# First tile in one DMA with its mean split over ScalarE and VectorE, and the third weight chunk loaded ahead of the third tile: a start-up change in a linear-attention and bilinear-GLU kernel

## The chip, the cores and the metric

The kernel runs on one core of one Trainium2 chip. The metric is the device time in microseconds (us) of one execution, as the median of several runs; the span in a profile, from the first to the last instruction, is 1.8 to 2.1 us shorter.

## The reference

Four layers follow one another on 2048 rows of 1024 bf16 values: linear attention (32 heads of 32), a bilinear GLU (inner width 3584), and both again, each on a layer-normalised input and added to its input. Only the first lines matter for the change: the layer norm of the first rows and the k part of the first product.

```python
def _layernorm(x, axis=-1, eps=1e-5):
    m = jnp.mean(x, axis=axis, keepdims=True)
    v = jnp.var(x, axis=axis, keepdims=True)
    return (x - m) / jnp.sqrt(v + eps)
...
    qkv = (x @ wqkv) ...            # x: [2048, 1024], wqkv: [1024, 3072]
    phi = lambda t: jnp.where(t > 0, t + 1, jnp.exp(t)) + 1e-6
    pq, pk = phi(q), phi(k)
...
    x = x + _A_ref(_layernorm(x, axis=-1), A_wqkv, A_wo)
    x = x + _B_ref(_layernorm(x, axis=-1), B_w_gate, B_w_up, B_w_down)
    # and the same two once more
```

## The kernel before

The rows are handled in 16 tiles of 128. `X[:, t, :]` is tile t, `wkv[:, k, :]` is chunk k (128 rows of the weight, 1024 columns). Every piece of the start is 256 KB: one tile of x or one chunk of the weight. All of them are issued by SyncE in this order; the first tile comes in two halves:

```python
    for c in range(2):
        load(X[:, 0, c * NB:(c + 1) * NB], x_view[:, 0, c * NB:(c + 1) * NB])
    load_x(1)
    for k in range(2):
        load_k(k, k + 1)
    load_x(2)
    for k in range(2, 4):
        load_k(k, k + 1)
    load_x(3)
    for k in range(4, 8):
        load_k(k, k + 1)
```

For the first four tiles the division by the standard deviation is put off to the exponential after the product, so TensorE needs only x minus its mean, turned round (the first three tiles are transposed on TensorE and copied out of PSUM, its output memory, by VectorE and ScalarE; the fourth by a DMA). `idle(9)` gives TensorE nine matmuls on zeros while nothing has landed. `k_part(t, a, b)` adds chunks a to b of tile t, two matmuls of 128x512 per chunk:

```python
            idle(9)
            ln_stats(0)                          # two bn_stats, bn_aggr on VectorE; rstd on GpSimd
            centre(0, stat[0][0][:, 0:1])        # x - mean on VectorE
            nc.scalar.activation(out=junk[:], in_=X[:, 1, :], func=ACT.Copy, scale=1.0 / D, accum_out=mean1[:])
            turn_pe(0, 2)
            take(nc.vector.tensor_copy, 0, 0, 0, 2)
            take(nc.scalar.copy, 0, 1, 2, 8)
            centre(1, mean1[:])
            k_part(0, 0, 1)
            turn_pe(1, 4)
            take(nc.vector.tensor_copy, 1, 0, 0, 4)
            take(nc.scalar.copy, 1, 1, 4, 8)
            ln_stats(2)
            centre(2, stat[2][0][:, 0:1])
            k_part(1, 0, 1)
            for k in range(1, 3):
                for t in range(2):
                    k_part(t, k, k + 1)
            turn_pe(2, 8)
            for t in range(2):
                k_part(t, 3, 4)
            take(nc.scalar.copy, 2, 0, 0, 8)
            ...                                   # tile 3, loads of the query weights and of tiles 4 to 15
            ln_stats(1)
            ...                                   # the other k parts, then three more layers
```

## Time and profile before

| | before |
|---|---|
| time, median of 3 runs | 1625.13 us (1624.67 to 1625.25) |
| span of the profiled run | 1623.0 us |
| TensorE busy | 1618.8 us |

These are lines of the page of the kernel before: its head, the line of busy time of TensorE and its neighbours, and the shares by engine of the chain that ended last.

```profile
span 1623.0 us, 18701 instructions
PE 1618.8 (100%) x8129; PEld 736.3 (45%) x8129; DVE 609.7 (38%) x895; ACT 287.4 (18%) x387; POOL 54.5 (3%) x136
PE 100%; DVE 0%; issue 0%
```

TensorE is the limit, and nothing else is. From about 10 us on its matmuls start 0.216 us apart (read up to 120 us). So all that a change of the start can win lies in the first 10 us. Here is the timeline of TensorE there, kernel before. The columns are start and duration in us, engine, line of the kernel, operation, output and inputs, shapes and how many instructions were merged; in brackets stands how long the engine sat idle before and what ended that. (The last line is cut off by the window.)

```profile
1.17 4.02 PE L172 MATMUL ps<-xT 128*128 128x512 bf16 x9 [1.17 <-DVE xT L167]
5.05 1.03 PE L408 MATMUL pt<-ident,R 128*128 128x128 bf16 x8
5.87 0.83 PE L202 MATMUL ps<-W,xT 128*128 128x512 bf16 x2
6.58 0.62 PE L408 MATMUL pt<-ident,R 128*128 128x128 bf16 x8
7.50 2.33 PE L202 MATMUL ps<-W,xT 128*128 128x512 bf16 x10 [0.30 <-DVE xT L411]
9.67 0.61 PE L408 MATMUL pt<-ident,R 128*128 128x128 bf16 x8
10.11 4.26 PE L202 MATMUL ps<-W,xT 128*128 128x512 bf16 x19
```

The three lines at L408 are the transposes of the first, second and third tile. Each transpose lasts longer than the distance to the next, since they are pipelined, so read starts: the last of the second tile's transposes starts at 6.98, a further one could start 0.056 us after it, and the next matmul starts at 7.50. That is a hole of 0.46 us, of which the profile counts 0.30 as idle. It waits for VectorE's copy of the second tile. Two smaller holes, about 0.06 us each, stand before the first and the second tile's transposes. Together they are 0.6 us.

VectorE's timeline of the same stretch, kernel before:

```profile
2.94 1.29 DVE L181 BATCH_NORM_STATS2 st<-X 128x6 f32<-128x512 bf16 x2 [1.82 <-DMA X<-in_A_x_dram]
4.26 0.21 DVE L183 BATCH_NORM_AGGREGATE mv<-st 128x2 f32<-128x12 f32 x1
4.51 0.48 DVE L395 TENSOR_SCALAR R<-X,mv 128x1024 bf16<-128x1024 bf16 x1
...
7.02 0.42 DVE L411 COPY xT<-pt 128x512 bf16<-128x512 bf16 x1 [0.49 <-PE pt L408]
7.37 1.29 DVE L181 BATCH_NORM_STATS2 st<-X 128x6 f32<-128x512 bf16 x2
8.69 0.21 DVE L183 BATCH_NORM_AGGREGATE mv<-st 128x2 f32<-128x12 f32 x1
8.93 0.49 DVE L395 TENSOR_SCALAR R<-X,mv 128x1024 bf16<-128x1024 bf16 x1
```

The first three lines are the first tile (its second half landed at 3.47), the last three the third tile, which landed at 7.34: statistics, aggregation, centring, ready at 9.42. TensorE arrived at the third tile's transposes at 9.67, so it did not have to wait for them, by a slack of only 0.2 us.

When a load has landed is read from its semaphore in the trace (the last of its 16 increments). Kernel before, in order of issue: first tile 2.92 and 3.47, second tile 4.83, chunk 0 5.70, chunk 1 6.66, third tile 7.34, chunk 2 8.48, chunk 3 9.14, fourth tile 9.82.

### The profile page before, as it was taken

The page shows a single profiled execution, that of the slowest core. Times are in us where ns is not written, and L with a number is a line of the kernel's source. Part 1 is how long each engine was busy: PE and PEld are TensorE (multiplying, and loading weights), DVE is VectorE, ACT ScalarE, POOL GpSimd, SP SyncE. Part 2 cuts the span into 40 slices and gives each one's busy share as a digit, 9 for nine tenths or more (in the row PEclk, how much of TensorE's full clock was granted, in tenths as well). Part 3 has the DMA queues.
Part 4 walks back from the last instruction along what each step waited for, and adds up shares of the span by engine and source line. Part 5 has one row for each costly group of instructions (what it writes and reads, how often), then busy time and mean ns, then how long its engine had stood idle before and what let it go on. Part 6 is the DMA issues. An engine that isn't in the chain of part 4 may idle for free.

```text
span 1623.0 us, 18701 instructions
## 1 busy us (share of the span) xinstructions
PE 1618.8 (100%) x8129; PEld 736.3 (45%) x8129; DVE 609.7 (38%) x895; ACT 287.4 (18%) x387; POOL 54.5 (3%) x136
## 2 busy tenths in 40 slices
PE   9999999999999999999999999999999999999999
PEld 4444444444444444444444444444444444444444
DVE  6889853212311321243245798432123113211111
ACT  5533201101110110011045222011011101101110
POOL 2100000000000000010000000000000000000000
PEclk9999999999999999999999999999999999999999
DMA  7324855511550452142420258555235306511400
GB/s 237 56 71 99 241 161 175 162 52 56 169 165 0 143 161 86 52 156 64 92 53 1 78 99 256 150 165 162 71 100 172 131 20 175 162 65 65 156 0 26
DMA packets 236065, 182.87 MB, mean 113 GB/s; under 512 B 101584, under 2 KB 216784, under 8 KB 235984
## 3 DMA queue, kind: packets, MB, share of 16 engines
q1 hardware_dynamic: 235984, 181.69, 38.8%
q8 instruction: 63, 1.03, 0.3%
q14 instruction: 18, 0.15, 0.0%
HBM read 153.09 MB, written 4.19 MB: 97 GB/s over the span
## 4 chain that ended last, share of the span: by engine, by line
PE 100%; DVE 0%; issue 0%
PE ps L202 50%; PE ps L526 48%; PE ps L553 1%; PE kv L310 0%; PE ps L172 0%; PE pm L334 0%; PE pt L408 0%; DVE xT L411 0%; DVE X L534 0%; DVE xT L167 0%; PE ps L334 0%
## 5 line engine op out<-in xcount | busy, mean ns | idle before, releaser
L526 PE MATMUL ps<-xT,R 128*128 128x512 bf16 x2432 | 528.5, 379 | 0.0
L526 PEld LDWEIGHTS <-R 128*128 128x128 bf16 x2432 | 238.0, 98 | 286.9
L530 DVE TENSOR_TENSOR R<-gs,ps 128x512 bf16<-128x512 f32 x224 | 153.9, 687 | 533.5 <-ACT gs L529 533.5
L202 PEld LDWEIGHTS <-R 128*128 128x128 bf16 x2248 | 219.9, 98 | 265.3
L529 ACT COPY gs<-ps 128x512 f32<-128x512 f32 x224 | 131.0, 585 | 1040.4 <-PE ps L526 1040.4
L526 PE MATMUL ps<-xT,W 128*128 128x512 bf16 x1152 | 251.6, 379 | 0.0
L202 PEld LDWEIGHTS <-xT 128*128 128x128 bf16 x1536 | 149.2, 98 | 180.0 <-issue 1.8
L202 PE MATMUL ps<-W,xT 128*128 128x512 bf16 x1024 | 225.3, 379 | 0.3 <-DVE xT L411 0.3
L526 PEld LDWEIGHTS <-W 128*128 128x128 bf16 x1152 | 112.7, 98 | 135.9
L202 PE MATMUL ps<-W,R 128*128 128x512 bf16 x744 | 170.7, 379 | 0.0
L534 DVE TENSOR_TENSOR X<-X,ps 128x1024 bf16<-128x1024 bf16 (+3 forms) x34 | 39.4, 1159 | 335.7 <-PE ps L202 326.1
L202 PE MATMUL ps<-R,R 128*128 128x512 bf16 x512 | 112.5, 379 | 0.0
L202 PE MATMUL ps<-PQ,R 128*128 128x512 bf16 x496 | 112.1, 379 | 0.0
L202 PE MATMUL ps<-R,xT 128*128 128x512 bf16 x512 | 110.8, 379 | 0.0
L181 DVE BATCH_NORM_STATS2 st<-X 128x6 f32<-128x512 bf16 x128 | 81.9, 682 | 2.4 <-DMA X<-in_A_x_dram 2.2
L207 ACT ACTIVATE e<-ps 128x1024 bf16<-128x1024 f32 x56 | 57.3, 1024 | 140.2 <-PE ps L202 140.2
L185 POOL TENSOR_SCALAR ve<-mv 128x1 f32<-128x1 f32 x64 | 16.7, 260 | 1328.7 <-DVE mv L183 1328.7
L202 PE MATMUL ps<-GL,R 128*128 128x512 bf16 x248 | 58.6, 379 | 0.0
L202 PE MATMUL ps<-xT,R 128*128 128x512 bf16 x248 | 58.6, 379 | 0.0
L379 DVE TENSOR_TENSOR X<-X,ps 128x1024 bf16<-128x1024 bf16 x32 | 38.5, 1212 | 25.9 <-PE ps L202 25.9
L192 DVE TENSOR_SCALAR R<-X,mv,rstd 128x1024 bf16<-128x1024 bf16 x64 | 33.9, 542 | 23.9 <-POOL rstd L187 23.9
L278 DVE TENSOR_TENSOR tmp<-PQ,GL 128x1024 f32<-128x1024 bf16 x32 | 39.0, 1220 | 6.4 <-ACT GL L271 6.3
(68 smaller groups left out, 436.1 us busy)
## 6 DMA issues: line engine op xcount, KB each, us to landing
R<-in_B_w_gate_dram SPq DMA_DIRECT2D x38, 1024.0 KB, 5.4
R<-in_B_w_up_dram SPq DMA_DIRECT2D x38, 1024.0 KB, 7.2
W<-in_B_w_gate_dram SPq DMA_DIRECT2D x18, 1024.0 KB, 5.3
W<-in_B_w_up_dram SPq DMA_DIRECT2D x18, 1024.0 KB, 7.3
W<-in_A_wqkv_dram SPq DMA_DIRECT2D x10, 1024.0 KB, 6.0
W<-in_B_w_down_dram SPq DMA_DIRECT2D x6, 1024.0 KB, 11.3
PQ<-in_B_w_down_dram SPq DMA_DIRECT2D x4, 1024.0 KB, 7.9
X<-in_A_x_dram SPq DMA_DIRECT2D x15, 256.0 KB, 5.4
```

The lines of the kernel that those rows point to most:

```text
L181: nc.vector.bn_stats(out=st[:, c, :], in_=X[:, t, c * NB:(c + 1) * NB])
L185: nc.gpsimd.tensor_scalar(out=ve[:], in0=mv[:, 1:2], scalar1=1e-5, scalar2=None, op0=ALU.add)
L192: nc.vector.tensor_scalar(out=dst, in0=X[:, t, :], scalar1=mv[:, 0:1], scalar2=rstd[:], op0=ALU.subtract, op1=ALU.mult)
L202: nc.tensor.matmul(out=ps[:, n, :], lhsT=lhsT, rhs=rhs[:, n * NB:(n + 1) * NB], start=start, stop=stop)
L207: nc.scalar.activation(out=e[:], in_=flat(ps), func=ACT.Exp, **sc)
L278: nc.vector.tensor_tensor(out=tmp[:], in0=q, in1=zacc, op=ALU.mult)
L379: nc.vector.tensor_tensor(out=X[:, t, :], in0=X[:, t, :], in1=flat(ps), op=ALU.add)
L526: nc.tensor.matmul(out=ps[:, n, :], lhsT=w[:, k, j * P:(j + 1) * P], rhs=xT[g % 2][:, k, :], start=(k == 0), stop=(k == KD - 1))
L529: nc.scalar.copy(out=gs[:], in_=ps[:, 0, :])
L530: nc.vector.tensor_tensor(out=hT[:, f, :], in0=gs[:], in1=ps[:, 1, :], op=ALU.mult)
L534: nc.vector.tensor_tensor(out=X[:, t, a:b], in0=X[:, t, a:b], in1=ps, op=ALU.add)
L553: nc.tensor.matmul(out=ps[:, 0, 0:b - a], lhsT=hT[:, f, tl * P:(tl + 1) * P], rhs=wd[f][:, a:b], start=(f == 0), stop=(f == KF - 1))
```

## The change

The intent is to let TensorE start its real work earlier. The first tile comes in one DMA instead of two, which also takes one issue out of the queue; its mean is summed in halves by ScalarE and VectorE side by side, and its full statistics are computed later, when only the exponential wants them. Chunks 1 and 2 of the weight are to be there earlier, and two matmuls of the first tile (chunk 1) are moved into the hole at 7.50.

```diff
--- before.py
+++ after.py
@@ -135,14 +135,12 @@
     def load_dn(j):
         load(dn[j], wd_v[:, 4 * j:4 * j + 4, :])
 
-    for c in range(2):
-        load(X[:, 0, c * NB:(c + 1) * NB], x_view[:, 0, c * NB:(c + 1) * NB])
+    load_x(0)
     load_x(1)
-    for k in range(2):
+    for k in range(3):
         load_k(k, k + 1)
     load_x(2)
-    for k in range(2, 4):
-        load_k(k, k + 1)
+    load_k(3, 4)
     load_x(3)
     for k in range(4, 8):
         load_k(k, k + 1)
@@ -413,9 +411,15 @@
             mean1 = small.tile([P, 1], F32, tag="mean1", bufs=1, name="mean1")
             junk = small.tile([P, D], BF16, tag="eb", bufs=3, name="junk")
 
+            half = small.tile([P, 3], F32, tag="half", bufs=1, name="half")
+
             idle(9)
-            ln_stats(0)
-            centre(0, stat[0][0][:, 0:1])
+            nc.scalar.activation(out=junk[:, 0:NB], in_=X[:, 0, 0:NB], func=ACT.Copy, scale=1.0 / D,
+                                 accum_out=half[:, 0:1])
+            nc.vector.tensor_reduce(out=half[:, 1:2], in_=X[:, 0, NB:D], axis=AX.X, op=ALU.add)
+            nc.vector.tensor_scalar(out=half[:, 2:3], in0=half[:, 1:2], scalar1=1.0 / D, scalar2=half[:, 0:1],
+                                    op0=ALU.mult, op1=ALU.add)
+            centre(0, half[:, 2:3])
             nc.scalar.activation(out=junk[:], in_=X[:, 1, :], func=ACT.Copy, scale=1.0 / D, accum_out=mean1[:])
             turn_pe(0, 2)
             take(nc.vector.tensor_copy, 0, 0, 0, 2)
@@ -427,10 +431,10 @@
             take(nc.scalar.copy, 1, 1, 4, 8)
             ln_stats(2)
             centre(2, stat[2][0][:, 0:1])
-            k_part(1, 0, 1)
-            for k in range(1, 3):
-                for t in range(2):
-                    k_part(t, k, k + 1)
+            k_part(0, 1, 2)
+            k_part(1, 0, 2)
+            for t in range(2):
+                k_part(t, 2, 3)
             turn_pe(2, 8)
             for t in range(2):
                 k_part(t, 3, 4)
@@ -441,6 +445,7 @@
             load_q()
             for t in range(4, NT):
                 load_x(t)
+            ln_stats(0)
             ln_stats(1)
             for t in range(2):
                 k_part(t, 4, 6)
```

## The prediction

> **What bounds the kernel.** TensorE. The page gives PE 1618.8 of 1623.0 us busy, and the chain of waits that ends last is 100% PE. From 10.1 us on, the timeline shows matmuls 0.216 us apart (over the first 60 us read) without a gap. The change touches only the first 12 us, so it can win only what PE idles there. By the starts in the timeline: about 0.06 us before the first tile's transposes (5.05 us), 0.06 us before the second tile's (6.58), and about 0.47 us before the matmul at 7.50, which waits for VectorE's copy of the second tile. In all 0.6 us, 0.04% of the span.
>
> **First tile.** Before: its second half is there at about 3.5 us, two statistics of 0.68 us, aggregation 0.21, centring 0.49, done at 4.99. After: I estimate the one DMA lands at 3.1; ScalarE's half takes about 0.65 plus 0.19 us for reading the accumulator (a whole row took 1.06 plus 0.19), VectorE's sum about 0.65 (a 512-wide statistic takes 0.68; the Trainium skill, "VectorE: DVE Perf Modes", lists `tensor_reduce` at the 1x rate only, which no run here shows yet), the combining operation 0.1, centring ends near 4.6. That is 0.4 us earlier, but worth only 0.06: the nine idle matmuls, 0.427 us each, hold PE until 4.99. The Trainium skill ("TensorE: Matmul & The Clock Gate", Part 1) says an idle PE starts at half clock; the trace agrees (0.427 us before about 6.3 us, 0.216 after).
>
> **Reordered matmuls.** The two matmuls of tile 0, chunk 1, move ahead of the wait at 7.50 and fill it (0.43 of 0.47 us). Chunk 1 landed at 6.66 and should now land near 6. With the second tile's transposes 0.1 us earlier, PE would reach the third tile's transposes near 9.1 instead of 9.67.
>
> **What gives it back.** The third tile is now sixth of the 256 KB pieces, not fifth. It landed at 7.34; VectorE needs 2.08 us from there (statistics, aggregation, centring), then PE transposes. The sixth piece landed at 8.48 before; one issue fewer (0.45 us each) and full-size packets bring it forward, and I estimate 7.65, between 7.3 and 8.1. Then its transposes start at about 9.75, against 9.67: PE idles 0.6 us there instead of at 7.5. Break-even is a landing at 7.56.
>
> **Moved.** The first tile's statistics now run after the third centring: rstd about 1 us later than its own need, so the first exponential starts near 14.4, not 13.83. PE does not wait for it. The second half of the query weights landed 22.96, wanted at 23.07: a gain above about 0.1 us needs the fourth tile's centring earlier too.
>
> **Sum.** -0.06 -0.06 -0.43 +0.6, so about 0: **1625.0 us, range 1624.2 to 1625.9**. Chances: faster by over 2% 0.00, within 2% 1.00, slower 0.00. The runs of before already differ by 0.6 us.
>
> **Right or wrong in the profile.** Right: the first transposes start at 4.95 to 5.05; no PE gap near 7.5; a new PE gap of 0.3 to 0.9 us before the third tile's transposes, ended by VectorE's centring, itself waiting for the DMA of the third tile. Wrong: no such gap (third tile landed by 7.2; then about 0.5 us gained), or the first transposes well before 4.9.
>
> **What would make it wrong.** A slow DMA engine that delays the third tile beyond 8.2 (time up to 1625.8); the moment the clock rises; a VectorE sum over 1 us.

## The result, and the profile after

| | before | after |
|---|---|---|
| median of 6 runs, same rounds | 1625.10 us (1624.67 to 1625.58) | 1625.24 us (1624.81 to 1625.38) |
| mean of the same runs | 1625.08 us | 1625.19 us |
| span of the profiled run | 1623.0 us | 1623.0 us |

A ratio is the mean time of one kernel's fast runs over that of the other's of the same rounds, so it is not quite the ratio of the medians quoted. Here it is 1.0001, with a 95% interval of 0.9988 to 1.0014: the same (a difference of less than 2% counts so).

TensorE's timeline after:

```profile
1.17 4.02 PE L170 MATMUL ps<-xT 128*128 128x512 bf16 x9 [1.17 <-DVE xT L165]
5.09 1.03 PE L406 MATMUL pt<-ident,R 128*128 128x128 bf16 x8
5.92 0.80 PE L200 MATMUL ps<-W,xT 128*128 128x512 bf16 x2
6.55 0.61 PE L406 MATMUL pt<-ident,R 128*128 128x128 bf16 x8
7.00 2.36 PE L200 MATMUL ps<-W,xT 128*128 128x512 bf16 x10
9.62 0.62 PE L406 MATMUL pt<-ident,R 128*128 128x128 bf16 x8 [0.27 <-DVE R L393]
10.08 4.26 PE L200 MATMUL ps<-W,xT 128*128 128x512 bf16 x18
```

The hole at 7.50 is gone: the ten matmuls start at 7.00, half a microsecond earlier. But the third tile's transposes start at 9.62, only 0.04 us earlier than before. A new wait stands there, ended by VectorE's line 393, which is the centring. (A matmul starts at 8.98, the next could start at 9.20; the hole is 0.43 us, 0.27 of it counted as idle.)

VectorE after, same stretch:

```profile
3.49 0.69 DVE L419 TENSOR_REDUCE half<-X 128x1 f32<-128x512 bf16 x1 [2.38 <-DMA X<-in_A_x_dram]
4.30 0.21 DVE L420 TENSOR_SCALAR half<-half 128x1 f32<-128x1 f32 x1
4.55 0.49 DVE L393 TENSOR_SCALAR R<-X,half 128x1024 bf16<-128x1024 bf16 x1
...
6.98 0.42 DVE L409 COPY xT<-pt 128x512 bf16<-128x512 bf16 x1 [0.77 <-PE pt L406]
7.52 1.29 DVE L179 BATCH_NORM_STATS2 st<-X 128x6 f32<-128x512 bf16 x2
8.84 0.21 DVE L181 BATCH_NORM_AGGREGATE mv<-st 128x2 f32<-128x12 f32 x1
9.08 0.48 DVE L393 TENSOR_SCALAR R<-X,mv 128x1024 bf16<-128x1024 bf16 x1
```

The first tile is centred at 5.03, not earlier than before (4.99): its one DMA landed at 3.47, just when the second half had landed. The third tile landed at 7.49 and its statistics start at 7.52.

The chain that ended last, followed back, says the same. These are the lines of the changed kernel from 3 to 10 us (start, duration, what):

```profile
3.06 4.44 DMA X<-in_A_x_dram
7.49 0.02 issue
7.52 1.30 DVE st L179 x2
8.81 0.02 issue
8.84 0.22 DVE mv L181
9.06 0.02 issue
9.08 0.50 DVE R L393
9.58 0.05 issue
9.62 0.62 PE pt L406 x8
```

Before, this chain ran through TensorE alone from 7.50 on:

```profile
7.50 2.33 PE ps L202 x10
9.83 0.45 PE pt L408 x8
```

Now it runs from the third tile's load through VectorE to the third tile's transposes.

A trap: in this profile the page gives TensorE 1610.7 us busy and 7978 matmuls, and the chain has an "issue" of 0.05 us every 10.8 us. That is not a loss. 151 of 8129 matmul records are missing, one in about 50; where one is missing, two starts stand 0.43 us apart.

### The profile page after: what moved, and what is told of

Read it like the earlier page. It is cut to its first block, busy times and chain, and to the rows that moved or that the text cites. A ratio compares the mean times of both kernels' runs of the same rounds, so it can differ in the third digit from the quotient of the medians.

```text
span 1623.0 us, 18555 instructions
## 1 busy us (share of the span) xinstructions
PE 1610.7 (99%) x7978; PEld 736.2 (45%) x8129; DVE 610.4 (38%) x897; ACT 288.3 (18%) x389; POOL 54.7 (3%) x136
## 4 chain that ended last, share of the span: by engine, by line
PE 99%; issue 1%; DMA 0%; DVE 0%; SPq 0%
PE ps L200 50%; PE ps L531 47%; PE ps L558 1%; PE kv L308 0%; DMA X<-in_A_x_dram 0%; PE pm L332 0%; SPq L110 0%; DVE st L179 0%; PE pt L406 0%; DVE R L393 0%; DVE X L539 0%; PE ps L332 0%; DVE mv L181 0%
```

## The experiments

Theory A: TensorE goes on when the third tile has landed and VectorE has centred it, so the time follows that landing (called the gate below). What is won earlier (first tile, order of the matmuls) is spent waiting there. Theory B: the time follows the first tile and the order of the matmuls, and the third tile has slack. Theory C: the differences are only scatter of the loads.

All profiles are collected in one table. "Start" is the start of the third tile's first transpose; "next" the start of the first matmul after these transposes.

| kernel | position of third tile | it lands | start | start minus landing | next | span minus next |
|---|---|---|---|---|---|---|
| before | 5th piece | 7.34 | 9.67 | 2.32 | 10.11 | 1612.85 |
| before_again | 5th | 7.51 | 9.72 | 2.21 | 10.17 | 1612.94 |
| matmul_order_only | 5th | 7.01 | 9.69 | 2.68 | 10.15 | 1612.96 |
| third_early | 5th | 7.93 | 10.07 | 2.13 | 10.53 | 1612.96 |
| after | 6th | 7.49 | 9.62 | 2.13 | 10.08 | 1612.95 |
| after_again | 6th | 8.11 | 10.24 | 2.13 | 10.70 | 1613.04 |
| after_timed | 6th | 8.26 | 10.39 | 2.13 | 10.84 | 1612.96 |
| old_matmul_order | 6th | 7.67 | 9.80 | 2.13 | 10.26 | 1613.03 |
| old_stats | 6th | 8.54 | 10.67 | 2.13 | 11.12 | 1612.91 |
| loads_only | 6th | 8.28 | 10.41 | 2.13 | 10.87 | 1612.93 |
| third_late | 7th | 8.44 | 10.57 | 2.13 | 11.03 | 1613.03 |
| third_halves | 6th | 7.65 | 9.26 | 1.61 | 9.72 | 1613.20 |
| third_halves_early | 5th | 7.35 | 9.16 | 1.80 | 9.60 | 1613.05 |
| best_two_loads | 5th | 8.04 | 9.65 | 1.61 | 10.11 | 1613.02 |

In eight profiles the start follows the landing by 2.13 us, to within 0.005 us. And the span minus "next" is the same in all but one profile, 1612.85 to 1613.05 us, so whatever moves that matmul moves the end by as much.

### after_again: the changed kernel, a second profile

No edit.

> The changed kernel once more, to see how much the early times move from profile to profile. Theory A (the third tile's landing plus VectorE's 2.08 us sets when PE goes on): the tile lands at 7.3 to 7.8, the third tile's transposes start 2.1 us after it (9.5 to 9.9), PE idles before them. Theory C (all is jitter of the DMAs): landing or restart moves by more than 0.4 us against the first profile (7.49 and 9.62).

Measured: one run, 1625.51 us; landing 8.11, start 10.24. TensorE's line of the third tile's transposes:

```profile
10.24 0.62 PE L406 MATMUL pt<-ident,R 128*128 128x128 bf16 x8 [0.82 <-DVE R L393]
```

The gap is as theory A has it, 2.13 us after the landing. But landing and restart moved by 0.62 us against the first profile, more than the 0.4 us that I had set for theory C. Both hold: the loads scatter, and the scatter goes through the gate. The first profile of the changed kernel happened to be a good one.

### third_late: third tile one piece later

```diff
-    for k in range(3):
+    for k in range(4):
         load_k(k, k + 1)
     load_x(2)
-    load_k(3, 4)
     load_x(3)
```

> The changed kernel with the third tile one piece later still (after weight chunk 3). Theory A: it lands near 8.16 instead of 7.49, the third tile's transposes start near 10.27 instead of 9.62, PE's gap before them grows from 0.43 (start to start beyond the 0.216 of a matmul) to about 1.1 us, and the run is 0.6 us longer. Theory B (the time follows the mean of the first tile and the order of the matmuls, the landing has slack): no change of the time, gap unchanged.

Measured: 4 runs, mean 1626.21 us (1625.84 to 1626.79), against 1624.91 for 7 runs of the kernel before in the same rounds: 1.3 us longer. By the verdict's 2% this too is the same, but each of the four lies above all seven (1624.51 to 1625.53). The tile landed at 8.44, the transposes started 2.13 us later:

```profile
10.57 0.62 PE L405 MATMUL pt<-ident,R 128*128 128x128 bf16 x8 [1.53 <-DVE R L392]
```

Theory B, which has no change of time here, falls. The size was as expected or above: 0.7 us more than the one run of the changed kernel.

### third_early: third tile where it was

```diff
-    for k in range(3):
+    for k in range(2):
         load_k(k, k + 1)
     load_x(2)
-    load_k(3, 4)
+    for k in range(2, 4):
+        load_k(k, k + 1)
     load_x(3)
```

> The changed kernel with the old load order (third tile before weight chunk 2): it lands near 6.87. Theory A in its simple form (landing plus 2.1 us): transposes of the third tile at PE's own arrival, 9.20, 0.43 us won. Theory A with VectorE in order: statistics can't start before its copy of the second tile ends at 7.40, so transposes at 9.50, only 0.12 us won against the changed kernel. Theory B: chunk 2 (landing now near 7.5) is what counts, and nothing is won or PE waits for it at 8.33 (it should not).

Measured: 4 runs, mean 1624.97 us, against 1624.91 before, and 1625.51 for the one run of the changed kernel. The times go with the position of the tile: 1624.97 as fifth piece, 1625.51 as sixth, 1626.21 as seventh. The profile missed every number that I had expected, since chunk 0 landed at 6.63 in this run and all later pieces with it; TensorE waited for that chunk, and the tile landed at 7.93. Two of TensorE's lines of it, the first matmuls and the third tile's transposes:

```profile
6.67 0.59 PE L201 MATMUL ps<-W,xT 128*128 128x512 bf16 x2 [0.86 <-DMA W<-in_A_wqkv_dram]
10.07 0.62 PE L407 MATMUL pt<-ident,R 128*128 128x128 bf16 x8 [0.16 <-DVE R L394]
```

Why chunk 0 was late can be read from the 16 increments of its semaphore, us from the span's start:

```
chunk 0 in third_early: 4.455 4.469 4.482 4.495 4.611 4.625 4.650 4.663 4.676 4.725 4.836 5.059 5.072 5.105 5.970 6.630
chunk 0 in after:       4.554 4.583 4.603 4.616 4.629 4.646 4.660 4.682 4.695 4.709 4.734 4.748 4.761 4.791 4.903 4.930
```

The Trainium skill ("DMA: Bandwidth & Descriptors", section "Why a DMA increments its semaphore by 16 and not by 1") says that up to 16 DMA engines carry one DMA and finish independently, and that only the full 16 means that all has landed. The trace agrees: 14 engines were done at 5.11, and the load counted as landed 1.5 us later because of two. What holds those two up, no run here shows.

### old_matmul_order: the changed kernel with the old order of the matmuls

```diff
-            k_part(0, 1, 2)
-            k_part(1, 0, 2)
-            for t in range(2):
-                k_part(t, 2, 3)
+            k_part(1, 0, 1)
+            for k in range(1, 3):
+                for t in range(2):
+                    k_part(t, k, k + 1)
```

> The changed kernel with the old order of the matmuls (tile 1's chunk 0 first). The gap after the second tile's transposes should come back (next matmul about 0.45 us after the last transpose, instead of 0.06). Theory A: PE then arrives at the third tile's transposes near 9.6, which is when they can start anyway, so their start stays 9.62 and the time within 0.1 us: the reordering is worth nothing behind this gate. Theory B: start moves to about 10.0, 0.4 us slower.

Measured: 4 runs, mean 1625.39 us (before 1624.91, the one run of the changed kernel 1625.51). The hole came back, and the gate still ruled (landing 7.67, start 9.80):

```profile
7.41 2.33 PE L200 MATMUL ps<-W,xT 128*128 128x512 bf16 x10 [0.29 <-DVE xT L409]
9.80 0.62 PE L406 MATMUL pt<-ident,R 128*128 128x128 bf16 x8
```

So the reordering, which does close a hole of 0.46 us, was worth nothing behind this gate. The start itself is 0.18 us later than the 9.62 expected, by as much as the tile landed later.

### loads_only: the kernel before with the new load order alone

```diff
-    for k in range(2):
+    for k in range(3):
         load_k(k, k + 1)
     load_x(2)
-    for k in range(2, 4):
-        load_k(k, k + 1)
+    load_k(3, 4)
     load_x(3)
```

> The kernel before with the one edit that weight chunk 2 is loaded ahead of the third tile. Theory A: the third tile lands later than the 7.34 of before, at about 8.0 to 8.5; its transposes start 2.13 us after the landing (the constant of five profiles so far), that is near 10.1 to 10.6 instead of 9.67; the run is 0.4 to 0.9 us longer than before. Theory B: no change, as chunk 2 was wanted first.

Measured: 4 runs, mean 1625.49 us, against 1625.09 before: 0.40 us longer, the low end of what theory A expected. Landing 8.28, and the transposes now wait:

```profile
10.41 0.62 PE L407 MATMUL pt<-ident,R 128*128 128x128 bf16 x8 [0.59 <-DVE R L394]
```

So the load order alone brings the wait; the longer time fits it, though the interval for this run (0.9988 to 1.0017) does not separate it from zero.

### matmul_order_only: the kernel before with the new order of the matmuls alone

The edit is the reverse of that in old_matmul_order, made in the kernel before.

> The kernel before with the new order of the matmuls alone. The wait of 0.30 us after the second tile's transposes goes. Theory A: the third tile's transposes start at the later of the landing plus 2.13 us (9.47 where it lands at 7.34) and PE's arrival (9.25, or later where chunk 2 is late): about 0.2 us won at most, nothing where the tile lands after 7.55. Theory B: 0.4 us won.

Measured: 4 runs, mean 1624.97 us, against 1625.09 before: 0.12 us less, within the scatter, and not the 0.4 us of theory B. In its profile the second tile's transposes happened to be late (6.82; the tile had landed at 5.07, not 4.83), so VectorE's copy of that tile was late too, and the start at 9.69 was bound by VectorE working in order, not by the landing at 7.01. This profile tells little about the gate.

### old_stats: the changed kernel with the first tile's mean from full statistics

```diff
-            nc.scalar.activation(out=junk[:, 0:NB], ..., accum_out=half[:, 0:1])
-            nc.vector.tensor_reduce(out=half[:, 1:2], in_=X[:, 0, NB:D], ...)
-            nc.vector.tensor_scalar(out=half[:, 2:3], in0=half[:, 1:2], ...)
-            centre(0, half[:, 2:3])
+            ln_stats(0)
+            centre(0, stat[0][0][:, 0:1])
 ...
-            ln_stats(0)
             ln_stats(1)
```

> The changed kernel with the first tile's mean taken as before, from the full statistics on VectorE. The one DMA lands near 3.45; two statistics, aggregation and centring end near 5.5 instead of 5.03, the first transposes start near 5.57 instead of 5.09. Theory A: most of this half microsecond is hidden behind the third tile, whose transposes still start 2.13 us after its landing (or at PE's arrival, near 9.7), so at most 0.1 us lost. Theory B: 0.45 us lost to the end.

Measured: 4 runs, mean 1625.53 us, against 1625.09 before. From the first tile's landing (3.35) to its transposes it took 2.13 us, where the halves take 1.62: the split is worth 0.5 us on its own path. It brought nothing: in this profile TensorE still sat idle 1.04 us at the third tile, which landed at 8.54:

```profile
5.48 0.62 PE L406 MATMUL pt<-ident,R 128*128 128x128 bf16 x8 [0.44 <-DVE R L393]
...
10.67 0.62 PE L406 MATMUL pt<-ident,R 128*128 128x128 bf16 x8 [1.04 <-DVE R L393]
```

The time differs from before as much as that of the changed kernel does (0.1 to 0.7 us), so no loss from the old statistics can be made out.

### after_timed: the changed kernel once more, timed

No edit.

> The changed kernel once more, timed together with the next two. Both theories: as before, within 0.3 us of the kernel before. Theory A adds: the third tile's transposes start 2.13 us after its landing, whatever the landing is in this profile, and span minus the start of the first matmul after them is 1612.9 to 1613.1 us.

Measured: 5 runs, mean 1625.72 us, against 1625.01 for 9 runs of before: 0.7 us longer, more than the 0.3 us expected. Landing 8.26, start 10.39, idle 1.32 us. Here the second tile's transposes started 0.30 us earlier than in the first profile (6.26 against 6.55) and the third tile's 0.76 us later, so the early part is not what counts:

```profile
6.26 0.61 PE L406 MATMUL pt<-ident,R 128*128 128x128 bf16 x8
10.39 0.62 PE L406 MATMUL pt<-ident,R 128*128 128x128 bf16 x8 [1.32 <-DVE R L393]
```

### third_halves: the same trick for the third tile

```diff
+            nc.scalar.activation(out=junk2[:, 0:NB], in_=X[:, 2, 0:NB], func=ACT.Copy, scale=1.0 / D,
+                                 accum_out=half2[:, 0:1])
             take(nc.scalar.copy, 1, 1, 4, 8)
-            ln_stats(2)
-            centre(2, stat[2][0][:, 0:1])
+            nc.vector.tensor_reduce(out=half2[:, 1:2], in_=X[:, 2, NB:D], axis=AX.X, op=ALU.add)
+            nc.vector.tensor_scalar(out=half2[:, 2:3], in0=half2[:, 1:2], scalar1=1.0 / D,
+                                    scalar2=half2[:, 0:1], op0=ALU.mult, op1=ALU.add)
+            centre(2, half2[:, 2:3])
 ...
             ln_stats(0)
             ln_stats(1)
+            ln_stats(2)
```

> The changed kernel with the third tile's mean taken by halves on ScalarE and VectorE too (its statistics moved after the fourth tile's centring). Theory A: the delay from the third tile's landing to its transposes falls from 2.13 us to 1.62 us (what the first tile's mean by halves takes from landing to transposes), so they start 0.5 us earlier for the same landing, down to PE's own arrival (2.64 us after the second tile's transposes start); the run is 0.3 to 0.5 us shorter than the changed kernel. Theory B: the VectorE work on the third tile is off the path; no change.

Measured: 5 runs, mean 1624.94 us, against 1625.72 for the changed kernel in the same rounds: 0.8 us less, more than the 0.3 to 0.5 expected (before: 1625.01). The delay from landing to start fell from 2.13 to 1.61 us. VectorE begins on the tile when it lands, and TensorE's transposes follow:

```profile
7.67 0.69 DVE L436 TENSOR_REDUCE half<-X 128x1 f32<-128x512 bf16 x1 [0.38 <-DMA X<-in_A_x_dram]
9.26 0.62 PE L406 MATMUL pt<-ident,R 128*128 128x128 bf16 x8
```

A next wait shows: one hole of 0.08 us at 11.09, for chunk 5. It is part of what sets 1613.20 apart in the table; the rest, some 0.1 us, was not located.

### third_halves_early: and the third tile ahead of chunk 2

The load order is that of third_early.

> The same with the third tile ahead of weight chunk 2, as in the old load order. Theory A: the transposes of the third tile start at PE's arrival, no gap before them, in profiles where the tile lands before about 7.5; 0.4 to 0.6 us shorter than the changed kernel and 0.3 us shorter than the kernel before. If the first weight chunk or the tile lands late by an engine that lags, as in some profiles so far, PE waits for that and the gain is smaller in that run. Theory B: no change.

Measured: 5 runs, mean 1624.51 us (1624.33 to 1624.68), against 1625.01 for 9 runs of before (1624.49 to 1625.54) and 1625.72 for the changed kernel. The ratio to before is 0.9997 with an interval of 0.9984 to 1.0009, so it is the same; but in one profile no idle time is left before the third tile's transposes, although chunk 0 was late and cost 0.44 us earlier:

```profile
6.09 0.59 PE L201 MATMUL ps<-W,xT 128*128 128x512 bf16 x2 [0.44 <-DMA W<-in_A_wqkv_dram]
6.52 0.61 PE L407 MATMUL pt<-ident,R 128*128 128x128 bf16 x8
6.96 2.36 PE L201 MATMUL ps<-W,xT 128*128 128x512 bf16 x10
9.16 0.61 PE L407 MATMUL pt<-ident,R 128*128 128x128 bf16 x8
```

The start, 2.64 us after the second tile's transposes began, is TensorE's own arrival. This version has the lowest mean of all; best_two_loads, below, equals it.

### before_again: how far equal kernels lie apart

No edit.

> The kernel before against itself: how far two equal kernels lie apart in five rounds, and a second profile of it. Both theories: means within 0.3 us. Theory A: the third tile lands near 7.0 to 7.5 (fifth piece), so PE reaches its transposes at 9.6 to 9.8 with no or a small gap; span minus the start of the first matmul after them is 1612.85 to 1613.05 us.

Measured: 5 runs, mean 1624.97 us, against 1624.98 for 9 runs of the same kernel: 0.01 us apart. Landing 7.51, start 9.72, no gap. Single runs of the kernel before range from 1624.4 to 1625.6 us.

### best_two_loads: third_halves_early with the first tile in two DMAs

```diff
-    load_x(0)
+    for c in range(2):
+        load(X[:, 0, c * NB:(c + 1) * NB], x_view[:, 0, c * NB:(c + 1) * NB])
     load_x(1)
```

> The fastest variant so far (third tile by halves and early) with the first tile loaded in two half DMAs again: what the single DMA is worth. Theory A: the second half lands at 3.4 to 3.5 as the single DMA does, so the first transposes start at 5.0 to 5.15 in both; one more DMA issue ahead of everything puts later pieces 0 to 0.45 us back; time within 0.2 us of the variant with one DMA (1624.5) and 0.3 to 0.5 us below the kernel before. Theory B: the single DMA carries the gain, and the time goes back to that of before.

Measured: 5 runs, mean 1624.53 us, against 1624.98 before. The second half landed at 3.43, the first transposes started at 5.05 (5.02 with one DMA). So the single DMA is worth nothing that can be measured in the time here. In this profile chunk 1 was late (7.37) and held TensorE up for 0.50 us.

## Why the prediction was right, and where it was off

- **The time and its reason held.** 1625.24 us lie in the range 1624.2 to 1625.9. That alone proves little, as the range reaches from a gain of 0.9 us, more than there was to win, to a loss of 0.8. The mechanism was the one foretold: the hole at 7.50 goes, and a new wait before the third tile's transposes takes its place, ended by the centring, which itself waits for the load. In starts of the first profile: second tile's transposes 0.03 us earlier, the matmul after them another 0.47 earlier, and 0.45 given back before the third tile, which leaves 0.04 us.
- **The first tile was mis-sized.** "I estimate the one DMA lands at 3.1 ... centring ends near 4.6" failed: it landed at 3.35 to 3.57 in all nine profiles with one DMA, and in the first of them the centring ended at 5.03. So not "-0.06" but +0.045 us, and it was not the nine idle matmuls that held TensorE, but the centring. The durations were right (half a row on ScalarE 0.63 and 0.19 us, VectorE's sum 0.69), except the combining operation, 0.21 us for one value per partition instead of 0.1. The first transposes started at 5.09, just outside "4.95 to 5.05".
- **The third tile's landing scatters.** "I estimate 7.65, between 7.3 and 8.1": the three profiles of the changed kernel have 7.49, 8.11 and 8.26; seven profiles with the tile as sixth piece have a mean of 8.00, six with it as fifth 7.53. The new gap, "0.3 to 0.9 us", was 0.43, 0.98 and 1.49 in starts (0.27, 0.82 and 1.32 counted as idle). The break-even that was named, a landing at 7.56, was met in the first of these three alone, so that the first call came out so near to zero is in part luck. The estimate had brought the sixth piece forward by 0.83 us, from 8.48. Over all profiles it lands at a mean of 8.37 with the first tile in two DMAs (five) and 8.01 with one (nine), 0.36 us apart, with overlapping ranges. Of the two reasons given, full-size packets show little: in the kernel before, 1 KB took 46 ns and 2 KB 84 ns (medians up to 12 us). So the term "+0.6" is on average larger, and the change is rather a small loss: 0.12, 0.60 (one run) and 0.71 us against before, with 0.01 us between two sets of the kernel before. The interval, over 0.1% wide, does not separate this from zero; the profiles, that of loads_only among them, show its cause.
- **What was said of the moved statistics was right in kind.** The first exponential started at 13.97 us in the first profile, not 14.4 (the fourth tile also landed earlier, 8.83 instead of 9.82), and at 14.58 and 14.72 in the other two; TensorE did not wait for it in any.
- **The rise of the clock** is a rival. The Trainium skill ("TensorE: Matmul & The Clock Gate", Part 1) puts the rise some 4 us into steady work and says that it varies; here it came 2.7 to 5.4 us after the first matmul. The profiles refute it for the wait at the third tile: seven of the eight with the delay of 2.13 us record the rise, at 3.89 to 6.35 us, and the delay does not change. In after_again it came at 3.89, in the first profile of the same kernel at 6.32, and yet after_again was 0.7 us longer.

Open are what delays single DMA engines at the start, and the last tenths of the mean difference between the two kernels.

## What to carry to other kernels

In a start-up where one engine is otherwise always busy, list for every load when it lands and what its consumer still has to do before the busy engine can go on; the latest of these gates decides, and work saved before it is only waited away. Before moving a load forward, ask what it moves back: here chunk 2 had to be in place at 8.8 us and was, at 8.5, while the third tile pushed back had 2.1 us of VectorE work behind it and a slack of 0.2. A speed-up pays at the gate: the mean by halves won nothing on the first tile and took 0.5 us off the delay of the third.

## What the Trainium skill lacked or had wrong

- "DMA: Bandwidth & Descriptors" (Latency and other measured facts) gives about 0.6 us to the first byte for DMAs issued from SyncE. It does not say from where it counts. Here the first packet came 1.02 to 1.15 us after the start of the first issue (0.72 to 1.75 in the changed kernel), but 0.62 to 0.76 us after its end, which fits.
- The same page says that the engines of a DMA finish independently, but not by how much. Here chunk 0, the third piece, issued at the same 1.64 us each time, landed between 4.93 and 6.63 us in the nine profiles with that order, up to 1.5 us after its fourteenth engine.
- "VectorE: DVE Perf Modes" (The perf-mode tier table) lists `tensor_reduce` at the 1x rate without a time. Elsewhere the page has general cycle formulas, but no measured time for an operation on one value per partition. Here 512 bf16 values took 0.69 us, as much as half of a row's statistics, and the [128, 1] operation 0.21 us.
- "TensorE: Matmul & The Clock Gate" (Part 1) gives about 4 us and 0.5 us of variation from run to run for the clock's rise, though further on it lets the number of slow matmuls in one kernel vary more than that. Over the 13 profiles of this start that record it, it came 2.7 to 5.4 us after the first matmul.
